# Tile-major storage of turned queries, keys and x, crossbar requests of two or three tiles, x of batch 2 by the crossbar, and a new written order

## The chip, the cores and the metric

The kernel runs on one core of a Trainium2 chip. The core has five engines that run their own instruction streams and meet at semaphores: TensorE (PE; its weight loads are shown apart as PEld), VectorE (DVE), ScalarE (ACT), GpSimd (POOL) and SyncE (SP). Work on data is done by the first three; here GpSimd and SyncE mostly issue DMA transfers. Everything an instruction touches lies in SBUF, the core's memory of 128 partitions, or in PSUM, eight banks into which TensorE writes. The metric is the device time of one run in microseconds.

## The reference

Attention with a window and a few global keys feeds a gated long convolution. Batch is 4, heads 8, sequence 768, head dimension 64, so the model width is 512.

```
scores = q k^T / 8 - slope[h] * dist        # keep = first 8 keys, or 0 <= i - j < 96
a      = softmax(where(keep, scores, -1e9)) # dist = 96 for a global key out of the window
x      = concat_heads(a v)                  # 4 x 768 x 512
x1, x2, x3 = split(x w_proj)                # 512 -> 3 * 512
x2     = irfft(rfft(x2) * rfft(filter))     # along the sequence, length 768
out    = (x1 * x2 * x3) w_out
```

## The kernel before

**Tiles of a batch.** The sequence is cut into seven key tiles. A key tile has 128 rows: 8 global keys and 120 keys of its own (`KL = 120`). Tile t's keys meet a band of at most 216 queries that begins at query 120 t; the widths are `EW`. Tiles are worked in three groups, `GRP = [(0, 1), (2, 3), (4, 5, 6)]`. Queries are loaded in six tiles of 128 rows. Four head pairs share the 128 partitions, 64 rows for each head of a pair, so that the scores of both heads run side by side on TensorE (`scores`, L798 to 835).

**Turning.** TensorE contracts over partitions, so queries, keys and the attention's result x have to be turned. This is done in three ways. For batch 0, `turned_pair` (L728) turns pairs of heads from contiguous loads. For batches 1 and 2, `turned` (L778) turns tile by tile on TensorE into a PSUM bank, and ScalarE or VectorE copies the bank into QT or KT. For batch 3, `crossed` (L764) has SyncE issue a DMA transpose (the crossbar) from SBUF to SBUF for each tile, 13 requests. x of batches 0 to 2 is turned on TensorE and copied out of PSUM, and x of batch 3 by 12 crossbar requests, two for each group and half of the heads (`transpose_x`, L895). `XB` and `XX` name the batches whose queries and keys, or whose x, go by the crossbar.

**Storage.** QT, KT and xT hold the head pair (or the chunk of 128 channels) as the outer dimension and the sequence inside it. xn, the attention's result before turning, is two buffers, one for each half of the heads.

**After the attention.** `gate` (L963) multiplies x with the first and last third of w_proj; for a batch whose x came by the crossbar its columns come in pieces of 120 out of tiles of 128 (L990, L993), for the others in 384 at a time (L988). `butterfly` (L920) folds x for the transform, `conv` (L1034) projects it (L1049), transforms it (`transform`, L705), multiplies it with the filter's spectrum (L1216 to 1234), transforms it back (L1136 to 1141), gates it and multiplies it with w_out (L1100); SyncE stores the result from one of six output buffers (L1107). The filter's spectrum is made once (`spectrum`, L635).

**Order.** The kernel first lists some 950 operations with what each reads and writes, and then issues them in an order written out in the string `ORDER`: number, engine letter (P, A, V, G for GpSimd, S for SyncE) and, for P, the PSUM banks. Each engine runs its part of that order strictly in sequence. Words such as `i1b0` are matmuls of no use that keep TensorE running in the front. The costs in `g.op(...)` were used to find such an order, and take no part in the run.

**Queues.** [...] SyncE issues stores, crossbar requests, and copies of the global rows within SBUF (`load_global`), in its own sequence.

Of the kernel before, what the change touches and what calls it, by code (L numbers as in the profile page):

```python
# [28 lines left out]
def act(n):  # L29
    return 0.06 + n / 1200.0  # L30
# [11 lines left out]
0V 34G 18S 30S i1b0 15V i1b0 21S 5G 35V i1b0 60V i1b0 59V 57V 10G 55V 7V i1b0 14V i1b0 24G 1V 56V 191A 8V i1b0 17V 61A  # L42
28G 190A i1b0 12A 20V i1b0 36V i1b0 19A 54V 58V 37G 214P0 13V 193A i1b1 29G 11V 215A i1b1 16V 192A i1b1 196A 25G 216V
204P1 22A 217V 38G 209P2 23V 26G 205A 219P0 39V 62V 63V i1b3 220A 52G 108P3 206V 210A 66P4 194A 207V 109A i1b5 27G
i1b5 211V 106P5 221V 42G 67V i1b1 i1b1 94P1 43G 212V 114P67 208A 110V 222V 92P4 213A 40G 95V i1b2 218A 111P23 223A
107A i1b0 41G 96V 64P0 93V i1b1 259G 115P 53V 224V 103P45 68V 65V 46G 195A 104P 112P 116A 80P1 199V 257G 9V 105A 81V
100P67 i1b0 i1b0 113A 101P 82V 225V 97P01 102A 6V 72P23 98P 232V 31A 73P 86P67 260G 99A 33S 117P45 226V 198V 74A 233V
78P0 118P 79A 75P23 234V 44G 76P 119A 32V 87P 235V 83P01 45G 77A i1b4 236V 69P45 256G 88A 70P 237V 84P 89P23 71A 258G
90P 238V 125P67 85A i1b4 227V 48G 126V 135P45 127V 91A 47G 120P01 136V 252P67 121V 267G 137V 130P23 253A 122V 241P4
254A 272G 138P5 131V 123P0 132V 249P67 266G 139V 352P1 251A 152P23 353V 273G 242A 133P7 250A 153V 157P45 268G 154V  # L50
124A 128P6 350P0 265G 158V 129A 155P1 159V 348P2 197A 354A 156A 49G 246P6 349V 160P4 351A 50G 244P5 134V 247A 161V
360P01 362P23 203V 271G 182V 361A 239P4 181V 140P67 274G 240A 175V 363A 174V 261G 143P01 177V 141A 202V 51G 245A
355P67 144V 275G 357P23 356A 377P5 375P4 176V 460G 358A 378V 414P6 165P01 184V 376A 264G 183V 415V 379A 277G 255V
380P45 385P67 381A 146P23 200V 185V 386A 178V 464G 142V 412P4 145V 186A 416P5 179V 162P67 476G 262S 180V 147A 417V
263S 413A 471G 148V 187V 387P23 418A 163A 149P45 359V 388A 243V 188V 289P6 270G 150A 189V 419P23 269G 290A 382P45 201V
279P7 151V 383A 389V 478G i1b6 420A 365P45 276G 281P6 166A 366V 367V 463G 280A 421P23 364V 426P01 282A 424P45 293P7
480G 422A 384V 283P6 425A 294V 461G 299P23 427A 167V 370P45 423V 477G 368P7 284A 171P01 369A 371V 472G 372V 300A
390P67 428V 462G 172A 395P45 164V 285P23 248A 469G 396V 173V 228P0 286A 391V 397V 291P1 470G 301V 229A 555P2 230A 392V
465G 434P45 292A 302V 231A 429P67 556A 468G 287V 168P01 430V 678G 557A 435V 431V 475G 551P2 436V 169A 373P3 553P6 664G
393P7 552A 374V 619P4 554V 398P5 295P01 394V 481G 620A 399V 580P2 288V 296A 563P45 663G 467S 565P67 581V 578P3 566A  # L60
466S 437P0 297V 667G 617P2 564A 170V 432P1 438V 686G 400P67 298V 618A 579V 682G 433A 309P2 567V 401A 681G 560P45
558P01 307P3 452V 310A 403P67 679G 561A 451V 685G 559A 305P2 402V 311P4 308A 453V 677G 303P5 404A 317P0 621V 454V
315P3 479G 306A 615P1 562V 406P67 318A 316A 670G 312A 616V 304A 455V 573P23 666G 407A 313P1 574V 405V 627P45 582A 456V
278G 314A 482P0 575V 628A 683G 408V 588P67 457V 483A 622P23 590P45 492P1 623A 474G 320V 319V 591A 409P23 665G 458V
493A 321V 674G 589A 459V 502P01 568P45 473G 322V 668S 503A 494P6 569V 323V 684G 410A 496P7 570V 495A 675G 324V 583P23
497A 624P45 592V 439P01 625A 676G 584A 504V 680G 585P45 626V 629P67 440A 571P2 484P3 673G 630A 411V 325V 498P01 586A
442P67 631V 762S 485A 326V 499A 486P3 760S 587V 443A 598P01 637P45 487A 599V 327V 761S 572A 445P67 600A 638V 639V 758S
488P23 441V 593P45 501V 489A 576P0 759S 333P1 328V 446A 632P23 594V 500V 334A 671S 595A 448P67 490V 669S 505V 784S
633V 336P1 444V 577A 634V 449A 640P4 601P0 491V 337A 768P23 596P5 641V 783S 769A 512P6 602V 508P7 597V 513A 765P01
509V 770P23 763P45 766A 786S 329V 635P6 506P7 771A 518P0 636V 510P1 785S 507V 764A 514P6 654V 606P23 511A 822S 519A  # L70
655V 515A 516P1 345P0 450V 517A 447V 821S 607A 772V 520P1 346A 794P67 787P23 608V 792P45 338S 521A 767V 342P0 793A
819S 656V 330P1 788A 522V 820S 778P45 343A 523V 603P23 331A 657V 795A 779V 658V 773P01 604A 612P67 332S 774V 780V 524A
672S 775V 339P4 613A 796V 828P01 340A 789P67 659V 825P23 605V 790A 341S 609P45 525V 829A 660V 526V 642P67 826A 781S
791V 4A 610A 823P23 776S 614V 830P01 3A 824A 611V 645P45 527V 831A 661V 782S 802P23 528V 643A 648P01 803V 529V 646A
335S 777S 804A 651P45 662V 644V 827V 797P67 649A 806S 700P2 798V 832V 799A 833P01 805S 647V 531V 689P3 701A 800S 702P6
# [1306 lines left out]
```

## Time and profile before

| what | us |
|---|---|
| median of 3 runs | 167.62 |
| lowest, highest run | 166.46, 171.16 |
| span of the profiled execution | 166.3 |
| busy: PE, DVE, ACT, POOL | 157.9, 151.4, 148.2, 73.8 |

The page of the profiled execution gives its span, from its first to its last instruction, and no other time of its own; the lowest of the runs is 0.2 us longer. The page has six parts: busy time by engine; the span in 40 slices; the DMA queues; the chain of work that ended last, followed back from the end; the costliest groups of instructions; and the DMA issues. In a row of a group stand the line of the kernel, the engine, the operation, what it writes and reads, the count, the busy time and the mean duration in ns, and then the idle time just before it with what ended it. Matmuls are pipelined: a row's duration of one matmul is longer than the distance between two, which the starts in the chain show.

### The profile page before, as it was taken

To read this page: it belongs to the slowest core of one execution; us is meant where nothing else is said; L and a number is where in the kernel's file an instruction comes from. 1 tells how busy PE (TensorE), PEld (TensorE's weight loads), DVE (VectorE), ACT (ScalarE), POOL (GpSimd) and SP (SyncE) were. 2 spreads that over 40 slices of the span, in tenths; PEclk is the share of its full clock that TensorE was granted. 3 is DMA by queue.
4 is the path that set the end of the run, shared out by engine and by line. 5 is a ranking of instruction groups with operands and counts; after the bars stand their busy time and mean duration, and the time that the engine had idled before them with its cause. 6 is when DMAs were issued, how large, how long until landed. Compare 5 with 4: busy or idle time off the path is not lost.

```text
span 166.3 us, 4460 instructions
## 1 busy us (share of the span) xinstructions
PE 157.9 (95%) x1735; PEld 98.2 (59%) x1735; DVE 151.4 (91%) x348; ACT 148.2 (89%) x268; POOL 73.8 (44%) x94
## 2 busy tenths in 40 slices
PE   6999998999999999999999999999999699999991
PEld 2356566856536687765566685566555454585440
DVE  6898699899979999999999999999999979999960
ACT  3999995998999979999999999999997579998972
POOL 7896399999699979999730000000000000000000
PEclk9999999999999999999999999999999999999999
DMA  5999999999999999999999656423133135000696
GB/s 151 146 138 194 160 161 153 170 170 176 175 162 149 152 148 125 137 145 139 159 152 144 122 97 155 85 79 110 40 73 112 68 129 189 0 4 0 252 348 221
DMA packets 90365, 22.84 MB, mean 137 GB/s; under 512 B 81504, under 2 KB 87016, under 8 KB 90344
## 3 DMA queue, kind: packets, MB, share of 16 engines
q0 software_dynamic: 74880, 12.46, 100.9%
q1 hardware_dynamic: 15464, 10.10, 22.2%
q8 instruction: 13, 0.21, 0.5%
q14 instruction: 8, 0.07, 0.1%
HBM read 25.69 MB, written 6.29 MB: 192 GB/s over the span
## 4 chain that ended last, share of the span: by engine, by line
PE 50%; DMA 16%; DVE 15%; POOL 13%; issue 2%; SPq 1%; ACT 1%; ACTq 0%; POOLq 0%; DVEq 0%
PE bank L988 10%; PE bank L1100 10%; PE bank L1049 7%; DMA g<-in_moe_filter_fft_dram 6%; PE bank L990 5%; POOL kn L330 4%; DMA vn<-in_v_dram 4%; POOL qn L330 4%; DMA vn<-vn 3%; PE bank L811 3%; DVE xn L885 2%; DMA out_dram<-ot 2%; PE bank L861 2%; DVE E L835 2%; PE bank L866 2%
## 5 line engine op out<-in xcount | busy, mean ns | idle before, releaser
L823 ACT ACTIVATE E<-bank 128x864 f16<-128x864 f32 x48 | 40.5, 909 | 1.2 <-PE bank L811 1.1
L988 PE MATMUL bank<-xT,w 128*128 128x384 f16 x192 | 34.7, 326 | 0.0
L318 ACT ACTIVATE x<-bank 128x768 f16<-128x768 f32 (+2 forms) x31 | 25.5, 830 | 2.4 <-PE bank L988 1.0
L330 POOL DMA_DIRECT2D vn<-in_v_dram x28 | 25.6, 923 | 2.2 <-DMA w<-in_moe_w_proj_dram 1.6
L988 PEld LDWEIGHTS <-w 128*128 128x128 f16 x192 | 17.7, 98 | 11.1 <-issue 0.3
L1100 PE MATMUL bank<-wo,y 128*128 128x512 f16 (+1 forms) x100 | 22.5, 370 | 0.0
L330 POOL DMA_DIRECT2D kn<-in_k_dram x24 | 21.8, 910 | 1.5 <-DMA wo<-in_moe_w_out_dram 1.0
L330 POOL DMA_DIRECT2D qn<-in_q_dram x21 | 18.4, 881 | 5.7 <-DMA g<-in_moe_filter_fft_dram 4.2
L835 DVE TENSOR_TENSOR E<-E,mask 128x1728 f16<-128x1728 f16 x18 | 18.8, 1048 | 0.0
L318 ACT ACTIVATE ot<-bank 128x512 f32<-128x512 f32 (+1 forms) x23 | 12.9, 599 | 3.5 <-PE bank L1100 1.8
L885 DVE TENSOR_TENSOR xn<-bank,rc 128x512 f16<-128x512 f32 (+1 forms) x20 | 15.5, 789 | 0.3
L861 PEld LDWEIGHTS <-E 128*128 128x128 f16 x224 | 14.1, 97 | 2.8 <-DVE E L835 0.7
L1049 PE MATMUL bank<-w,xab 128*128 128x512 f16 x64 | 15.6, 379 | 0.0
L861 PE MATMUL bank<-vn,E 128*128 128x65 f16 x224 | 15.3, 193 | 0.2 <-DMA vn<-vn 0.2
L1100 PEld LDWEIGHTS <-y 128*128 128x128 f16 x100 | 9.5, 98 | 10.0 <-issue 0.3
L866 PE MATMUL bank<-vn,E 128*128 128x65 f16 x192 | 15.1, 193 | 0.0
L314 ACT CAST ab<-bank 128x512 f16<-128x512 f32 x23 | 13.7, 607 | 0.7 <-PE bank L1049 0.6
L866 PEld LDWEIGHTS <-E 128*128 128x128 f16 x192 | 13.2, 97 | 0.9
L811 PE MATMUL bank<-QT,KT 64*128 64x216 f16 (+2 forms) x224 | 13.3, 241 | 0.4 <-DVE pp L1229 0.4
L314 ACT CAST eo<-bank 128x384 f16<-128x384 f32 x30 | 12.9, 523 | 0.5 <-PE bank L1141 0.5
L314 ACT CAST X<-bank 128x1024 f16<-128x1024 f32 x12 | 12.2, 1032 | 0.0
L811 PEld LDWEIGHTS <-KT 64*128 64x128 f16 x224 | 7.9, 94 | 6.6 <-issue 5.2
(187 smaller groups left out, 363.0 us busy)
## 6 DMA issues: line engine op xcount, KB each, us to landing
out_dram<-ot SPq DMA_DIRECT2D x23, 256.0 KB
vn<-in_v_dram POOLq DMA_DIRECT2D x28, 120.0 KB, 6.1
kn<-in_k_dram POOLq DMA_DIRECT2D x21, 120.0 KB, 6.4
qn<-in_q_dram POOLq DMA_DIRECT2D x18, 128.0 KB, 6.1
w<-in_moe_w_proj_dram POOLq DMA_DIRECT2D x4, 256.0 KB, 6.8
g<-in_moe_filter_fft_dram POOLq DMA_DIRECT2D x1, 768.0 KB, 10.6
kn<-in_k_dram POOLq DMA_DIRECT2D x3, 192.0 KB, 4.3
qn<-in_q_dram POOLq DMA_DIRECT2D x3, 192.0 KB, 5.0
```

The costliest lines, as they stand in the source:

```text
L314: {"A": nc.scalar.copy, "V": nc.vector.tensor_copy, "G": nc.gpsimd.tensor_copy}[e](out, in_)
L318: self.nc.scalar.mul(out, in_, c)
L330: return self.g.op(eng, 0.57 + 0.00035 * nbytes[0] if eng == "G" else 0.5, lambda _: e.dma_start(dst, src), w=w, r=r, nbytes=nbytes, name= ...
L811: nc.tensor.matmul(bs[hh].f32()[:, off:off + w], self.KT[hs, hp, P * m:P * m + P], self.QT[hs, hp, KL * m:KL * m + w], start=(off == 0 and ...
L823: g.op("A", act(864), lambda _: nc.scalar.activation(eo, bs[0].two()[:, :, 0:432].rearrange("p h (m w) -> p h m w", m=2), Act.Exp, scale=s ...
L835: g.op("V", dve(1728, 2), lambda _: nc.vector.tensor_mul(ep, ep, mk), r=[("mask", h) for h in range(hs.start, hs.stop)] + ([("mask0", hp - ...
L861: nc.tensor.matmul(o[:, n, hh], ef[:, at:at + P], vt[:, t, 2 * hp + hh, 0:D + 1], start=first, stop=(t == 0), skip_group_check=True)
L866: nc.tensor.matmul(o[:, n, hh], ef[:, at:at + P], vt[:, t - 1, 2 * hp + hh, 0:D + 1], start=False, stop=True, skip_group_check=True)
L885: nc.vector.tensor_mul(to, o[:, :, :, 0:D], rc.to_broadcast([P, 2, 2 * nt, D]))
L988: nc.tensor.matmul(bk.f32()[:, 0:h], w, self.xT[:, c, lo:lo + h], **kw)
L1049: nc.tensor.matmul(bk.f32(), src[:, c], w[:, c, DM:2 * DM], start=(c == 0), stop=(c == 3))
L1100: nc.tensor.matmul(bk.f32()[:, 0:n], y[:, c, P * t:P * t + P], self.wo[:, c, ns], start=(c == 0), stop=(c == 3))
```

## The change

- QT, KT and xT get the tile as the outer dimension, then the head pair or chunk, then 128 columns. xn becomes one buffer with the tile outside and all heads inside.
- Queries are loaded in seven tiles that begin every 120 rows and overlap by eight (the last has 48 rows), as the key tiles do. A score of 216 columns then reads two query tiles, 120 and 96 columns, in two matmuls. Batches 1 and 2 turn a seventh query tile. Batch 0's copies of turned queries are split in two instructions.
- A crossbar request covers all tiles of a group: three requests for queries (3, 2, 2 tiles) and three for keys (2, 2, 3) of batch 3.
- x of batch 2 goes by the crossbar too (`XX = (2, 3)`); for each group one request takes both halves of the heads. TensorE's transposes of it and the copies go; its gates and butterfly read tiles of 120 columns. As batch 1 has stored x in the other layout, the requests of batch 2 are put after all readers of batch 1's x (`past`).
- h1, half of whose slots were unused, shrinks from six to four.
- `ORDER` is written anew: 931 operations in place of 949, 88 on GpSimd in place of 85, 49 on SyncE in place of 62, 20 useless matmuls in place of 26. In it the load of the filter stands at place 58 of GpSimd's entries (it was the 11th), the spectrum comes after five of batch 0's projections, and attention of batches 1 and 2 comes earlier against the convolution of batch 0.

```diff
 ORDER = """
...
-    XX = (3,)
+    XX = (2,3)
+    QG = [(0, 1, 2), (3, 4), (5, 6)]
...
-        self.qn = t("qn", [P, 6, H, D])
+        self.qn = t("qn", [P, 7, H, D])
-        self.QT = t("QT", [P, 4, S])
-        self.KT = t("KT", [P, 4, 7 * P])
+        self.QT = t("QT", [P, 7, 4, P])
+        self.KT = t("KT", [P, 7, 4, P])
-        self.xn = [t(f"xn{i}", [P, 2, 7, 2, D]) for i in range(2)]
-        self.xTt = t("xT", [P, 4, 7, P])
-        self.xT = self.xTt.rearrange("p j t c -> p j (t c)")[:, :, 0:S]
+        self.xn = t("xn", [P, 7, 4, 2, D])
+        self.xTt = t("xT", [P, 7, 4, P])
+        self.xT = self.xTt.rearrange("p t j c -> p (t j c)")[:, 0:4 * S].rearrange("p (j s) -> p j s", j=4)
...
     def load_q(self, b, t):
-        src = self.q[b, :, P * t:P * t + P, :].rearrange("h p d -> p h d")
-        self.load("G", self.qn[:, t], src, [("qn", t)], (1024, 256), f"q{t}")
+        n = min(P, self.S - KL * t)
+        src = self.q[b, :, KL * t:KL * t + n, :].rearrange("h p d -> p h d")
+        self.load("G", self.qn[0:n, t], src, [("qn", t)], (8 * n, 256), f"q{t}")
...
     def crossed(self, what, ts, buf):
-            o, i = dst[:, :, P * t:P * t + P], buf[:, t].rearrange("p h d -> p (h d)")
+        o = (self.QT if what == "q" else self.KT)[:, ts[0]:ts[-1] + 1].rearrange("p t i c -> p (t i) c")
+        i = buf[:, ts[0]:ts[-1] + 1].rearrange("p t h d -> p (t h d)")
...
             for m in m0:
-                w = self.EW[m]
-                for hh in range(2):
-                    hs = slice(64 * hh, 64 * hh + 64)
-                    nc.tensor.matmul(bs[hh].f32()[:, off:off + w],
-                                     self.KT[hs, hp, P * m:P * m + P],
-                                     self.QT[hs, hp, KL * m:KL * m + w],
+                for x, w in ((m, min(KL, self.EW[m])), (m + 1, self.EW[m] - KL)):
+                    for hh in range(2 if w > 0 else 0):
+                        hs = slice(64 * hh, 64 * hh + 64)
+                        nc.tensor.matmul(bs[hh].f32()[:, off:off + w], self.KT[hs, m, hp],
+                                         self.QT[hs, x, hp, 0:w],
...
         if self.b in self.XX:
-            for i in range(2):
-                g.op("S", 0.3 + 0.25 * len(ts), lambda _, i=i: nc.sync.dma_start_transpose(
-                    out=self.xTt[:, 2 * j + i, ts[0]:ts[-1] + 1],
-                    in_=self.xn[j][:, i, ts[0]:ts[-1] + 1].rearrange("p t h d -> p (t h d)")),
+            if j == 0:
+                if c == 0:
+                    ks = [("xT", x, y, i) for x in range(2) for y in range(3) for i in range(2)]
+                    self.past = {o for k in ks for o in g.readers.get(k, ())} if self.b - 1 not in self.XX else set()
+                return
+            g.op("S", 0.3 + 0.25 * len(ts), lambda _: nc.sync.dma_start_transpose(
+                out=self.xTt[:, ts[0]:ts[-1] + 1].rearrange("p t i c -> p (t i) c"),
+                in_=self.xn[:, ts[0]:ts[-1] + 1].rearrange("p t i h d -> p (t i h d)")),
+                r=[("xn", 0, c), ("xn", 1, c)], w=[("xT", x, c, i) for x in range(2) for i in range(2)],
+                nbytes=(128 * len(ts), 1024), name="crossx", after=self.past)
             return
```

More of the change, by code (lines that the diff above doesn't have):

```diff
@@ L47 @@
[L47 to L51, printed above, removed]
@@ L691, in packed @@
         g.op("P", 2 * pe(512), run, acq=[b, b2], r=keys + ["twin"], name="fwd")
-        g.op("AV", self.evac(512), lambda e: self.times(e, h1[:, s], b.f32(), sc), use=[b],
+        g.op("AV", self.evac(512), lambda e: self.times(e, h1[:, s - 2], b.f32(), sc), use=[b],
              w=[("h", s, 1)])
@@ L780, in turned @@
         b = g.bank()
+        rows = [min(P, self.S - KL * t) if what == "q" else P for t in ts]
         def turn(_):
@@ L912, in run @@
                     o = step * i + KL * n
-                    nc.tensor.transpose(tx[:, o:o + P], self.xn[j][:, i, t], self.ident)
-        g.op("P", 0.0559 * 2 * len(ts), run, acq=[b], r=[("xn", j, c), "ident", "xpad"], name="trx")
+                    nc.tensor.transpose(tx[:, o:o + P], self.xn[:, t, 2 * j + i], self.ident)
+        g.op("P", 0.0559 * 2 * len(ts), run, acq=[b], r=[("xn", j, c), "ident"], name="trx")
         dst = self.xT[:, 2 * j:2 * j + 2, self.Q0[c]:self.Q0[c] + W]
```

174 lines of the change are left out of this document (91 added, 83 removed).

## The prediction

> **What bounds the kernel now.** I read the page first, then the chain of work that ended last, then the stretches of 10 us, and last the rows of the lines that the diff touches.
>
> ```profile
> span 166.3 us, 4460 instructions
> PE 157.9 (95%) x1735; PEld 98.2 (59%) x1735; DVE 151.4 (91%) x348; ACT 148.2 (89%) x268; POOL 73.8 (44%) x94
> PE 50%; DMA 16%; DVE 15%; POOL 13%; issue 2%; SPq 1%; ACT 1%; ACTq 0%; POOLq 0%; DVEq 0%
> ```
>
> The chain is TensorE for half of the span, and DMA and GpSimd for 29%. VectorE and ScalarE are busy for 91% and 89%, so there is no engine on which work can be put for nothing. The stretches say where each of these binds (columns: stretch, length, then busy time and count of PE, PEld, DVE, ACT, POOL, clock, DMA share, GB/s):
>
> ```profile
> 0.00:10.00 10.00, 8.59 (x67) 3.45 (x69) 7.57 (x44) 7.28 (x18) 8.66 (x22) 1.00 0.82 150
> 20.00:30.00 10.00, 9.19 (x173) 6.94 (x168) 9.44 (x23) 7.97 (x13) 9.82 (x12) 1.00 2.14 160
> 80.00:90.00 10.00, 10.00 (x122) 6.47 (x121) 9.96 (x17) 10.00 (x21) 3.32 (x4) 1.00 2.58 144
> 130.00:140.00 10.00, 8.49 (x53) 4.27 (x52) 8.43 (x16) 7.78 (x17) 0.00 (x0) 1.00 0.31 114
> ```
>
> GpSimd, which issues every load, is nearly full in the front and done before 90 us; in the middle PE, DVE and ACT are all full; and from 130 to 140 us PE lacks 1.5 us. That hole has a name:
>
> ```profile
> 126.98 0.57 SPq L1107 DMA_DIRECT2D out_dram<-ot  x1
> 130.91 0.60 ACT L318 ACTIVATE ot<-bank 128x512 f32<-128x512 f32 x1 [1.69 <-DMA out_dram<-ot]
> ...
> 114.30 12.63 SPq L900 DMA_TRANSPOSE xT<-xn  x9
> ...
> L900 SPq DMA_TRANSPOSE xT<-xn x12: 1180/1200/2282, 109.8 to 125.7; - x12
> L773 SPq DMA_TRANSPOSE QT<-qn x6: 1193/1214/1306, 85.5 to 100.9; - x6
> PE bank L1139 <- ACT ot L318: 1.5, 1, 1.5
> ```
>
> SyncE issues nine crossbar requests of x in one row, 12.63 us, and a store that stands behind them goes out only at 126.98. ScalarE waits 1.69 us for its buffer, and TensorE 1.5 us for ScalarE.
>
> **The change on TensorE.** It is the engine of the chain in the middle and at the end, so I sum it there. The rows (start, time, what):
>
> ```profile
> 61.32 0.22 PE bank L913 x4
> 98.31 1.30 PE bank L988 x8
> 135.45 0.15 PE bank L990
> 135.63 0.16 PE bank L990
> 142.05 1.22 PE bank L990 x8
> 60.88 0.45 PE bank L785 x8
> ...
> 111.21 0.55 PE L811 MATMUL bank<-QT,KT 64*128 64x216 f16 x12
> L811 PE MATMUL bank<-QT,KT x224: 181/252/263, 14.0 to 111.6; 64*128 64x216 f16 x80, 64*128 64x168 f16 x16, 64*128 64x48 f16 x16
> ```
>
> *Removed:* the 28 transposes of x of batch 2 (seven tiles by four). Four take 0.22 us, so 28 take 1.54 us.
>
> *Gates of batch 2.* Eight gates of eight matmuls of 384 columns are 8 x 1.30 = 10.40 us. In the crossbar's layout four are of 360 columns, 4 x 1.22, and four have 360 and 48: from one 360 to the next are 0.18 us (135.45 to 135.63), so eight are 1.42. Together 4.88 + 5.68 = 10.56 us: +0.16.
>
> *Scores.* A score of 216 columns becomes one of 120 and one of 96, because a query tile now holds 120 used columns. Per head 13 matmuls stand for 7, so 6 x 32 = 192 more, which run in pairs: 96 more pairs, the same columns. From 384 to 360 columns a matmul falls from 1.30/8 = 0.1625 to 1.22/8 = 0.1525 us, 2.4 columns per ns. The 12 scores at 111.21 are six pairs of 216, 168, 48, twice; from the first start to the last are 0.55 - 0.18 = 0.37 us, over five pairs of 816 columns, 0.34 us. What is left is 6 ns a pair. 360 columns at that rate are 0.150 of the 0.1525 us, so 2.5 ns is the low end. 96 pairs cost 0.24 to 0.58 us; I take 0.4, between.
>
> *The seventh query tile.* Batches 1 and 2 turn 48 rows more, four transposes each. At most that is a full transpose, 0.45/8, for eight: 0.45 us; at least the 48 columns of the gate, 0.18 - 0.15: 0.2 us. I take 0.2, the row of that width.
>
> TensorE together: -1.54 + 0.16 + 0.4 + 0.2 = **-0.8 us**.
>
> **Beside TensorE.** For the middle:
>
> ```profile
> L314 DVE COPY xT<-bank 128x480 f16<-128x480 f16 x7 | 2.7, 399 | 0.2 <-PE bank L913 0.2
> L314 ACT COPY xT<-bank 128x480 f16<-128x480 f16 x5 | 3.0, 605 | 0.4 <-PE bank L913 0.3
> L931 DVE TENSOR_TENSOR xab<-xT 128x1536 f16<-128x1536 f16 x4 | 3.6, 951 | 0.0
> L935 DVE TENSOR_TENSOR xab<-xT x2: 751/752/752, 128.2 to 129.2; 128x1152 f16<-128x1152 f16 x2
> L936 DVE TENSOR_TENSOR xab<-xT x2: 299/300/302, 128.9 to 129.9; 128x288 f16<-128x288 f16 x2
> L937 DVE TENSOR_TENSOR xab<-xT x2: 200/200/201, 129.1 to 130.1; 128x96 f16<-128x96 f16 x2
> L314 DVE COPY QT<-bank 128x512 f16<-128x512 f16 x2 | 0.8, 418 | 0.0
> ```
>
> Six copies of x out of PSUM go, 6 x 0.40 on DVE or 6 x 0.605 on ACT: 2.4 to 3.6 us. The butterfly of batch 2 reads three pieces instead of one: 2 x (0.752 + 0.300 + 0.200 - 0.951) = +0.6. Two small query copies come, at most 2 x 0.42, and four copies of batch 0 are split, each with a second instruction near that of L937: +0.8 both times. So 0.2 to 1.4 us less on two engines together; I count it at nothing, since PE's own work covers it. If it did not, it would be a gain. The writes of xn get another order of dimensions, which no row shows; I take zero, and 20 such writes a tenth longer would be 1.6 us.
>
> **The crossbar.** Requests fall from 25 to 12: six for queries and keys of batch 3, three for x of batch 2, three for x of batch 3. A request now covers two or three tiles, 8 to 12 blocks of 128x128, while the rows have 2 or 3 blocks at a median of 1.200 us and 4 blocks at 1.214. Twice the blocks cost 1% more. So I take 1.2 to 1.3 us each, 15 us of SyncE in place of 31; the other end is 0.3 us per block. Each request waits for its last tile and, for x, for both head groups. All three x requests of batch 2 stand behind the last gate of batch 1, which is new (`past`):
>
> ```profile
> 82.27 0.40 PE L913 MATMUL bank<-ident,xn 128*128 128x128 f16 x4
> 91.23 1.46 PE L988 MATMUL bank<-xT,w 128*128 128x384 f16 x8
> ```
>
> Now x of batch 2 starts to be turned at 82.27, though batch 1's last gate runs only until 92.69. Behind these requests on SyncE stand the two copies of global value rows of batch 3 and then the stores of batch 0; values of batch 3 and the output buffers wait for them. Three requests are 3 x 1.25 = 3.8 us after the gate; the order puts all of batch 1's gates ahead, and other batches' matmuls cover it. Nothing is counted. Of the 1.5 us hole at 130 us I count **-1.0**: stores no longer stand behind nine requests, but what is late next there is the butterfly and its projection.
>
> [...]
>
> **The front.** The written order moves the 1.5 MB load of the filter from the 11th of 85 to the 58th of 88 of GpSimd's entries, and with it the spectrum: seven DVE steps, six transforms with their copies. GpSimd also gets three query loads.
>
> ```profile
> 8.27 10.61 DMA g<-in_moe_filter_fft_dram
> ...
> 3.41 1.76 POOL L330 DMA_DIRECT2D kn<-in_k_dram  x2
> ...
> 19.41 0.90 POOL L330 DMA_DIRECT2D qn<-in_q_dram  x1 [4.23 <-DMA g<-in_moe_filter_fft_dram]
> L330 POOL DMA_DIRECT2D qn<-in_q_dram x21: 629/906/1069, 6.1 to 82.7; - x21
> L690 PE MATMUL bank<-g,p x4: 376/378/379, 26.6 to 28.6; 128*128 128x512 f16 x4
> ```
>
> GpSimd stalls 4.23 us behind the filter now, ahead of batch 1's loads; that much the front can gain. The three loads add at most 3 x 0.906 = 2.7 us, the last of them behind everything that waits early. Against it, the spectrum's vector work leaves a front where DVE has 2.4 us of room in 10 and goes where it has 0.04. Ends: -4.2 and +6 (below). I take 0, for the same work is only done at another time.
>
> **Sum.** -0.8 - 1.0 + 0 = -1.8 us on the profiled execution, 164.5. Its span is 166.3; the runs are 166.46 to 171.16, median 167.62, so a run lies 0.2 to 1.3 us over it without the highest. With 0.7 that gives **165.2 us**, 1.4% under the median. Own range 163.3 to 167.0. Two per cent is about what a measurement of this kernel tells from no change.
>
> **Rivals.**
>
> *The front gets shorter* (0.26). Loads of batches 0 and 1 come up to 4.2 us sooner, TensorE starts its attention sooner, and the stall behind the filter meets a time when loads are ahead. The row of 4.23 speaks for it; that PE's busy time in the front includes filler matmuls, so it has room, does too. With 3 of the 4.2 us: 165.2 - 3 = 162.2.
>
> *The filter comes too late* (0.24). This is the slower side. Ahead of it stand 52 loads at 0.9 us and 3.4 us of setup (first load at 3.41): issued at about 50 us, landed 10.6 later, at 60. Now the first transform runs at 26.6, 7.7 us after the landing at 18.9, so then it would be at 68. The matmuls that the order puts ahead of it (attention of batches 0 and 1, scores of 2, five projections) are, by my count of the order, about what PE has done now some 0.7 us after it turns x of batch 1 at 61.32, say by 62. PE, in order, would stand 6 us, and DVE has no room to catch up: 165.2 + 6 = 171.2. It decides as soon as the six transforms start later than PE is through, by the load or by the sums on DVE. Against it: the sums need not take 7.7 us.
>
> *Requests cost by the block* (0.08). Then x of batch 2 adds 28 blocks at 0.3, 8.5 us of SyncE ahead of values of batch 3, the 1.0 us does not come, and x lands 2 us later per group of three tiles: 165.2 + 1.0 + 1 = 167.2.
>
> **How the numbers follow.** The forecast has 0.42. Under 164.3 (2% under 167.62) lie the shorter front and 0.04 of the forecast: 0.30. Over 171.0 lies most of the late filter: 0.20. The rest, 0.50, is within 2%. The range leaves out the far part of the two outer rivals: 161.5 to 171.0.
>
> **What would show it.** Right: no L913 after 70 us; crossbar requests on SyncE of 1.2 to 1.3 us whatever their tiles; no wait of ScalarE for a store past 120 us; PE's busy time by matmuls about 1 us less. Front: the stall on the filter gone from GpSimd's waits, first scores before 14 us. Wrong: transforms of the spectrum that wait for DVE or the filter, a request of 2.4 us or more, values of batch 3 waiting for their global rows, or PE waiting for an x copy. Longer xn writes would also make it wrong.

## The result and the profile after

The changed kernel is slower: 175.12 us (median of 4 runs, 174.8 to 175.57) against 167.04 for the kernel before on the same chip; the ratio is 1.056, with a 95% interval of 1.051 to 1.062. The forecast was 165.2. The profiled execution of the changed kernel took 175.57 us; its span is 173.8 against 166.3, so there are 7.5 us to find. (Runs of one kernel fall into a faster and a slower group; the ratios compare the faster runs, and where a trace is of a slower one, as those of no_v3, new_xx3, v_after and store_first are, only waits and starts are read from it.) Three rows and the clock of the page after:

```profile
span 173.8 us, 4867 instructions
PE 161.2 (93%) x1933; PEld 102.0 (59%) x1933; DVE 151.1 (87%) x346; ACT 151.0 (87%) x271; POOL 75.6 (43%) x97
PEclk9999999999999999999987999999999999999997
PE 41%; POOL 27%; DMA 22%; issue 5%; DVE 2%
```

In the chain of work that ended last, TensorE has 41% instead of 50%, and GpSimd and DMA together have 49% instead of 29%. VectorE and ScalarE are busy for 151.1 and 151.0 us, against 151.4 and 148.2 before, in a longer span. So the kernel waits more for data, and the clock row says that TensorE was slowed near the middle. The stretches find the place (columns as before: stretch, length, busy time and count of PE, PEld, DVE, ACT, POOL, then clock, DMA share, GB/s):

```profile
85.00:90.00 5.00, 1.30 (x12) 0.57 (x9) 4.86 (x10) 1.59 (x4) 0.90 (x1) 1.00 1.80 89
90.00:95.00 5.00, 4.87 (x62) 2.97 (x63) 0.00 (x0) 3.52 (x5) 0.00 (x0) 0.66 1.83 144
130.00:140.00 10.00, 10.00 (x76) 5.95 (x75) 9.87 (x20) 8.84 (x17) 0.00 (x0) 1.00 0.42 116
```

From 85 to 90 us TensorE works for 1.30 us of 5; before, the stretch from 80 to 90 was full. From 90 to 95 it is busy, but at a granted clock of 0.66. From 130 to 140, where the kernel before lacked 1.5 us, it is now full. The waits name what was missing at 85:

```profile
PE bank L815 <- DMA QT<-qn: 3.8, 1, 3.8
PE bank L815 <- DMA KT<-kn: 1.5, 1, 1.5
```

Scores (L815) wait for turned queries and turned keys, which are those of batch 3, the batch that goes by the crossbar. The timeline, SyncE's requests first and then two rows of scores, shows when they were asked for and when they were used:

```profile
72.77 1.34 SPq L774 DMA_TRANSPOSE KT<-kn  x1
74.28 4.54 SPq L774 DMA_TRANSPOSE QT<-qn  x1
78.99 5.20 SPq L774 DMA_TRANSPOSE KT<-kn  x1
84.35 8.81 SPq L774 DMA_TRANSPOSE QT<-qn  x2
93.32 4.73 SPq L774 DMA_TRANSPOSE KT<-kn  x1
99.67 6.88 SPq L908 DMA_TRANSPOSE xT<-xn  x3
...
63.33 0.59 PE L815 MATMUL bank<-QT,KT 64*128 64x96 f16 x18
90.13 0.46 PE L815 MATMUL bank<-QT,KT 64*128 64x120 f16 x6 [3.83 <-DMA QT<-qn]
```

The last scores of batch 2 are done by 63.9 us; the first of batch 3 come at 90.13. The same places in the timeline of the kernel before, with its first request:

```profile
81.79 0.55 PE L811 MATMUL bank<-QT,KT 64*128 64x216 f16 x10
83.71 1.66 SPq L773 DMA_TRANSPOSE KT<-kn  x1
94.51 0.36 PE L811 MATMUL bank<-QT,KT 64*128 64x216 f16 x4 [0.39 <-DVE pp L1229]
```

There batch 2's scores end at 82.3 and batch 3's begin at 94.51, with a wait of 0.39 us that is not for a transfer. The rows of the lines that the change touches (minimum, median and maximum in ns; first and last start in us):

```profile
L774 SPq DMA_TRANSPOSE KT<-kn x3: 1341/4728/5202, 72.8 to 93.3; - x3
L774 SPq DMA_TRANSPOSE QT<-qn x3: 3004/4542/5636, 74.3 to 90.2; - x3
L908 SPq DMA_TRANSPOSE xT<-xn x6: 1233/1410/2955, 99.7 to 131.1; - x6
L922 PE MATMUL bank<-ident,xn x56: 217/219/230, 28.9 to 63.1; 128*128 128x128 f16 x56
L815 PE MATMUL bank<-QT,KT x416: 179/203/298, 13.7 to 112.0; 64*128 64x120 f16 x63, 64*128 64x96 f16 x54, 64*128 64x48 f16 x22
```

Requests of queries and keys take 3 to 5.6 us, but for the first. The three of x of batch 3, past 120 us, when no load moves, take 1.23 to 1.25 us for two tiles and 1.40 for three. And the chain of after steps over exactly this stretch:

```profile
77.70 15.59 DMA vn<-in_v_dram
93.32 11.97 DMA KT<-kn
```

A load of v issued at 77.70 lands 15.6 us later (the median of such loads on the page is 6.5), and the last key request, begun at 93.32, lands 12 us later.

**A balance of TensorE's work.** I add up the matmuls by their starts, at the distance that the prediction found (columns at 2.4 per ns, and 2.5 ns), without the useless ones. The sum is 141.1 us before and 140.4 after.

```
us           before   after   difference
up to 85      67.2     64.7     -2.5      the front
85 to 110     23.6     16.9     -6.7      the crossbar stage
110 to end    50.3     58.8
whole        141.1    140.4     -0.7
```

In the span: 2.5 behind at 85 us, less 0.7 that need not be done, is 1.8; plus 6.7; minus 1.0 that comes back later, where the hole at 130 us was (from 110 us to the end of the span 56.3 us for 50.3 of work before, 63.8 for 58.8 after): +7.5. The two waits of the crossbar stage, 3.8 and 1.5 us, and the 1.7 that a clock of 0.66 costs in 5 us make 7.0, near the 6.7 of the table. At its first scores of batch 3 the kernel before has 65.1 us of work left, and the changed one 74.5: TensorE begins these scores 4.4 us sooner, with 9.4 us more still to do. It asks for their queries sooner still, at 86.30 us, when its wait begins, against 94.51.

### The profile page after: what moved, and what is told of

It reads as the page before. It is cut to its first block, busy times and chain, and to the rows that moved or that the text cites. A ratio compares the mean times of both kernels' runs of the same rounds, so it can differ in the third digit from the quotient of the medians.

```text
span 173.8 us, 4867 instructions
## 1 busy us (share of the span) xinstructions
PE 161.2 (93%) x1933; PEld 102.0 (59%) x1933; DVE 151.1 (87%) x346; ACT 151.0 (87%) x271; POOL 75.6 (43%) x97
## 4 chain that ended last, share of the span: by engine, by line
PE 41%; POOL 27%; DMA 22%; issue 5%; DVE 2%
PE bank L999 11%; PE bank L1113 10%; POOL kn L329 9%; DMA vn<-in_v_dram 9%; POOL vn L329 9%; POOL qn L329 8%; DMA KT<-kn 7%; DMA w<-in_moe_w_proj_dram 6%; PE bank L1062 6%; PE bank L309 4%; PE bank L704 2%; PE bank L1152 1%; PE bank L864 1%; PE bank L869 1%; PE bank L1002 1%
## 5 line engine op out<-in xcount | busy, mean ns | idle before, releaser
L329 POOL DMA_DIRECT2D vn<-in_v_dram x28 | 26.5, 959 | 5.7 <-DMA qn<-in_q_dram 4.7
L1113 PE MATMUL bank<-wo,y 128*128 128x512 f16 (+1 forms) x100 | 23.4, 371 | 0.1
L999 PE MATMUL bank<-xT,w 128*128 128x360 f16 x128 | 23.3, 314 | 0.0
L997 PE MATMUL bank<-xT,w 128*128 128x384 f16 x128 | 23.0, 326 | 0.3 <-ACT x L317 0.2
L329 POOL DMA_DIRECT2D qn<-in_q_dram x24 | 20.7, 877 | 4.6 <-DMA w<-in_moe_w_proj_dram 2.4
L815 PE MATMUL bank<-QT,KT 64*128 64x120 f16 (+2 forms) x416 | 15.6, 210 | 5.4 <-DMA QT<-qn 3.8
L815 PEld LDWEIGHTS <-KT 64*128 64x128 f16 x416 | 11.1, 96 | 11.9 <-issue 8.6
L997 PEld LDWEIGHTS <-w 128*128 128x128 f16 x128 | 11.9, 98 | 7.8
L999 PEld LDWEIGHTS <-w 128*128 128x128 f16 x128 | 12.2, 97 | 7.1
L313 ACT CAST ab<-bank 128x512 f16<-128x512 f32 x24 | 14.4, 625 | 1.8 <-PE bank L1062 1.8
L1062 PE MATMUL bank<-w,xab 128*128 128x512 f16 x64 | 15.6, 382 | 0.2 <-ACT xT L313 0.2
L864 PEld LDWEIGHTS <-E 128*128 128x128 f16 x224 | 13.9, 97 | 1.4
```

Source lines behind the costliest of these rows:

```text
L313: {"A": nc.scalar.copy, "V": nc.vector.tensor_copy, "G": nc.gpsimd.tensor_copy}[e](out, in_)
L329: return self.g.op(eng, 0.57 + 0.00035 * nbytes[0] if eng == "G" else 0.5, lambda _: e.dma_start(dst, src), w=w, r=r, nbytes=nbytes, name= ...
L815: nc.tensor.matmul(bs[hh].f32()[:, off:off + w], self.KT[hs, m, hp], self.QT[hs, x, hp, 0:w], start=(off == 0 and not near), stop=True, sk ...
L864: nc.tensor.matmul(o[:, n, hh], ef[:, at:at + P], vt[:, t, 2 * hp + hh, 0:D + 1], start=first, stop=(t == 0), skip_group_check=True)
L997: nc.tensor.matmul(bk.f32()[:, 0:h], w, self.xT[:, c, lo:lo + h], **kw)
L999: nc.tensor.matmul(bk.f32()[:, 0:360].rearrange("p (t r) -> p t r", t=3), w, self.xTt[:, 3 * s:3 * s + 3, c, 0:KL], skip_group_check=True, ...
```

## The experiments

The theory to begin with: in the new order the requests run **beside loads**, and the two slow each other (*clash*). The rivals: a request of two or three tiles is slow by itself (*size*); the new order costs its time whatever the transfers do (*order*). What the trace holds of DMA packets, counted by start over 2 us, shows the first of these plainly:

```
kernel        us       load packets   crossbar descriptors (mean ns)
before        84-86       2401             19  (18)
before        86-88       1375            340  (34)
before        90-92         25           1638  (25)
after         72-74       2395              0
after         76-78        222            479  (59)
after         82-84        254            257  (54)   230 of the loads are 1 KB, of w_out
after         86-88        325            303 (136)
after        106-108         0           2016  (18)
```

One tile is 512 descriptors of 256 bytes. Alone, loads go at 2400 packets in 2 us and a request at some 2000 descriptors; from 86 to 88 us in the changed kernel, together, each goes at about a seventh of that. When the first request starts, 5,202 load packets are still to come before, and 13,559 after. The last of them starts at 90.4 us before, and at 104.7 after. The kernel before had the clash too, for four microseconds.

**old_order**: the changed code, in the order of before.

```diff
-5G 0V 15A 14V 7V 13V ...
+0V 34G 18S 30S i1b0 15V ...      (before's words, renumbered; a request after its last tile)
```

> The changed code with the order of the kernel before: the same storage, merged requests, x of batch 2 by the crossbar and seven query tiles, but every operation at its old place (a merged request at the place of its last part, the new ones beside their neighbours). Clash theory (crossbar requests and loads in flight together slow each other): requests start after the last load is issued, so each takes 1.2 to 1.6 us of SyncE, and the sum of the prediction holds: span 163.5 to 167, ratio 0.98 to 1.00. Size theory (a request of 8 to 12 blocks is slow by itself, or x of batch 2 by the crossbar comes too late): requests of 3 us or more, span 169 to 175. Order theory (the late filter and the new order of everything cost it): as the clash theory in the time, but with the front alone to blame, to be told apart by the other runs.

171.13 us, ratio 1.031 (1.018 to 1.044). SyncE's timeline:

```profile
85.01 5.14 SPq L775 DMA_TRANSPOSE QT<-qn  x1
90.25 0.71 SPq L330 DMA_DIRECT2D vn<-vn  x1
91.01 0.69 SPq L330 DMA_DIRECT2D kn<-kn  x1
93.36 1.24 SPq L909 DMA_TRANSPOSE xT<-xn  x1
94.72 1.83 SPq L775 DMA_TRANSPOSE QT<-qn  x1
```

The first request of queries, issued while loads run, takes 5.14 us; those from 93.36 on take 1.2 to 1.8. TensorE waits 2.5 us for queries, until 97.21. The order is not the whole loss. The 0.98 to 1.00 that the clash theory gave did not come: two requests still begin while loads run, and the last load is through only at 95.7 us. From 91.7 to 93.36 SyncE stands still: x of batch 2 is at the head of its queue and not ready, with queries and keys behind it.

**no_v3**, **by_tile** and **cross_late** change the new order's transfers: the first leaves out the seven loads of v of batch 3, the second splits each request of queries or keys by tile, the third lists batch 3's v as something a request reads.

```diff
+            if b == self.B - 1: (no load)                                        # no_v3
-   nc.sync.dma_start_transpose(out=o, in_=i)
+   for x in range(n): nc.sync.dma_start_transpose(out=o[:, 4 * x:4 * x + 4],    # by_tile
+                                                  in_=i[:, 512 * x:512 * x + 512])
-   r=[(what + "n", t) for t in ts] + ...
+   r=[(what + "n", t) for t in ts] + ... + [("vn", 1, t) for t in range(7)]     # cross_late
```

> The changed kernel without the seven loads of the values of batch 3 (its result for batch 3 is computed with the values of batch 1); order unchanged. These are the loads in flight beside the requests for queries and keys. Clash theory: requests of 1.2 to 2 us, TensorE's waits for QT and KT (5.3 us) nearly gone, clock 1.0, span 165 to 168. Size theory: requests stay at 3 to 5.6 us, span 172 to 174. Order theory: span 171 to 173.

> The changed kernel with each request for queries and keys of batch 3 issued as one request for each tile (14 in place of 6), at the same place. Size theory: requests back to 1.2 us each, queries land by 86, span 167 to 170. Clash theory: the 14 requests together take as long as the six (28 us of SyncE) or a little longer, span 173 to 177.

> The changed kernel, in which the requests for queries and keys of batch 3 wait until the seven loads of values of batch 3 have landed; the rest of the order as it was. Clash theory: the last load lands at 88 to 92 in place of 105, requests take 1.2 to 1.4 us, all keys and queries land by 100 in place of 105; TensorE waits longer for the first and not for the last, span 171 to 174. Size theory: requests of 3 us or more from 90 on, span 180 and more.

no_v3: two runs, 167.2 and 173.64 us, too few for a ratio; the trace is of the longer. In it requests still take 3.0 to 5.6 us until 88.9, as long as other loads run, but for the first; behind that all take 1.23 to 1.43. The span of the shorter run, 165.5 us at a clock of 1.00, lies where the clash theory put it, but it is one run. by_tile: 173.21, ratio 1.042 (1.019 to 1.066); its 14 requests take 1.2 to 2.8 us, and TensorE waits 4.3 us for queries. So *size* is out: the same tiles one by one come no sooner. cross_late: 173.4, ratio 1.043 (1.025 to 1.062). The list of what an operation reads sets only the order of issue, and as no data are shared, SyncE did not wait: the first request stands at 72.63 as ever. It tested nothing but issuing v a little earlier, and serves as a second look at the changed kernel: requests of 3.4 to 4.8 us, a wait of 2.8.

**fence_new** and **fence_old** make SyncE really wait, by a small copy that reads the seven tiles of v.

```diff
+        def sent(_):
+            if what == "k" and ts[0] == 0:
+                nc.sync.dma_start(self.fence, self.vn[1][NG:NG + 1, :, 0, 0:4])
+            nc.sync.dma_start_transpose(out=o, in_=i)
```

> The changed kernel, but SyncE first copies four values of each of the seven v tiles of batch 3 into a scratch row, ahead of its first crossbar request, so that no request starts before the last load has landed; GpSimd issues these seven loads ahead of their old places. Nothing is left out. Clash (requests and loads in flight at once slow each other): the last load lands before 92 us, the requests begin there and take 1.2 to 1.5 us each, whatever their tiles, all six are through 10 us after the fence; TensorE then waits for the last of them instead of for slow ones, and the time is 171 to 174 us. Size (a request of two or three tiles is slow by itself): each still takes 3 to 5 us behind the fence, 175 us or more. Order alone (the new order costs it whatever the transfers do): requests as with clash, but 175 us.

> The changed code in the order of before (171.1 us in its run) with the same fence ahead of the first request; nothing is left out. Clash: the query request that took 5.14 us there, begun at 85 us when the last load landed at 95.7, is gone, all requests take 1.2 to 1.5 us, the last load lands at 89 to 91 us as before, and the time falls by the 2 to 3 us that TensorE waited for queries: 168 to 169.5 us. Size: a request of queries stays above 3 us and the time at 171. If the fence puts the requests too late (they begin at 91 in place of 83), clash by its price alone: 171 again, but with requests of 1.2 us.

fence_new: 178.41 us, ratio 1.056 (1.045 to 1.068). SyncE's timeline, the wait and three stretches:

```profile
88.07 1.35 SPq L778 DMA_TRANSPOSE KT<-kn  x1
89.53 1.46 SPq L778 DMA_TRANSPOSE QT<-qn  x1
92.88 2.65 SPq L778 DMA_TRANSPOSE QT<-qn  x2
```

```profile
PE bank L820 <- DMA QT<-qn: 8.4, 1, 8.4
```

```profile
85.00:90.00 5.00, 0.17 (x1) 0.00 (x0) 3.70 (x7) 0.59 (x1) 0.00 (x0) 0.75 0.50 48
90.00:95.00 5.00, 1.47 (x25) 1.20 (x26) 0.00 (x0) 0.53 (x1) 0.00 (x0) 0.50 1.03 194
95.00:100.00 5.00, 5.00 (x46) 2.62 (x45) 1.02 (x2) 3.82 (x6) 0.00 (x0) 0.72 0.80 150
```

The transfers did as *clash* says: the last load at 86.7 instead of 104.7, requests of 1.3 to 1.7 us, all six landed by 98.8. The time did not: it is no better, because now TensorE stands 8.4 us until 93.53. My price was wrong; I had taken the requests to be ready before TensorE asked. fence_old: 174.52 us in the middle of four runs (172.46 to 176.79); the two shortest, 172.46 and 173.39, are too few for a ratio with an interval. The slow query request is gone (1.47 us in place of 5.14), but it starts at 93.49 instead of 85.01, and TensorE waits 2.9 us for queries and 1.8 for ScalarE. By these two, about 1.03 times the kernel before on that chip, a clash avoided by waiting costs as much as the clash (old_order: 1.031).

**filter_early**: only the filter's load goes back to its old place.

```diff
-... 49G 37G 48G ...   52G (58th)
+... 49G 52G 37G 48G ...
```

> The changed kernel with the load of the filter back at the 11th place of GpSimd's entries and all else in the new order; nothing is left out. If the moved filter cost the front its 2.5 us (TensorE had 64.7 us of work done at 85 us where before had 67.2), 172.5 to 173.5 us. If the front pays for other loads that now stand later, the filter ahead of them makes it worse: 176 to 178 us. If the front is no matter beside the crossbar stage: 175.

172.34 us, ratio 1.019 (1.007 to 1.031). The middle of the runs that the ratio compares, 172.02 us, over that of the kernel before on the same chip, 167.38, is 1.028, inside this interval but well above its middle. TensorE waits for a query load early, and not for queries in the crossbar stage:

```profile
PE bank L787 <- DMA qn<-in_q_dram: 2.7, 1, 2.7
```

```profile
85.00:90.00 5.00, 5.00 (x95) 4.10 (x94) 4.96 (x12) 4.48 (x11) 0.00 (x0) 1.00 1.69 148
90.00:95.00 5.00, 5.00 (x71) 3.08 (x64) 4.93 (x9) 4.71 (x8) 0.00 (x0) 1.00 2.68 114
```

The front is not faster, it is slower: by 85 us TensorE has done 3.4 us less than in the changed kernel. Its requests are as slow (2.8 to 5.7 us, but for the first). But TensorE comes to batch 3's scores when they can be had (89.69 us), with no idle stretch and a clock of 1.00. What it loses is lost early and not a second time. So the number came near one expectation (172.5 to 173.5) and its reason did not hold.

**probe** measures the disputed cost by itself: four one-tile requests in the kernel before, where only loads run.

```diff
+                    for i in range(4):
+                        self.nc.sync.dma_start_transpose(
+                            out=self.h1[:, 1 + 2 * (i % 2)]..., in_=self.fwd[:, 4:8]...)
```

> The kernel before, with four requests more of SyncE behind its copies of the global rows of batch 1, near 47 us, each turning 128 x 512 values of a constant into slots of h1 that nobody reads; nothing is left out. In that stretch loads run alone, at some 2,400 packets in 2 us, and no request stands beside them in the kernel before. Clash: each of these one-tile requests takes 2.5 to 5 us in place of 1.2, and the loads fall to below 1,200 packets in 2 us as long as they run; what is lost of 8 to 12 us of loads comes later, the last load lands 3 to 8 us after 90.4, and the kernel takes 169 to 174 us. If requests and loads do not slow each other: 1.2 us each, loads unchanged, 167.5 us.

168.96 us, ratio 1.012 (1.006 to 1.018), just under the range. Its packets over 2 us:

```
us       load packets   crossbar descriptors (mean ns)
46-48       2440              0
48-50       1018            390  (46)
50-52       1126            505  (43)
54-56       2424              0
56-58       1025            473  (48)
58-60       1334            531  (30)
```

Loads fall to less than half, and two tiles take more than 4 us to move, where 1024 descriptors alone would take one (an estimate, from the 2016 in 2 us above). The four cost about 5,300 load packets, 4.4 us at 2400 in 2 us; the last load starts 2.9 us later, where 3 to 8 were expected. But SyncE's rows are 1.2 to 1.6 us each, not the 2.5 to 5 that I expected: the row of one tile is **not** the time until it lands. Longer rows are, in the changed kernel, those of larger requests beside loads (3 to 5.6 us), and in by_tile those of some one-tile requests behind others (up to 2.8 us).

**old_xx3**, **new_xx3** and **old_qk_first** take x of batch 2 apart from the rest: off the crossbar in the order of before, off it in the new order, and behind all queries and keys in the order of before.

```diff
-    XX = (2,3)
+    XX = (3,)                        # old_xx3, new_xx3
-757S 756S ... 578S 775S 600S 638S 776S 806S 807S
+757S 756S ... 775S 776S 806S 807S 578S 600S 638S   # old_qk_first
```

> Storage by tile and requests of two or three tiles alone: the changed code with x of batch 2 turned on TensorE again (XX is batch 3 only), in the order of before. Nothing is left out. If the loss of the run in the order of before (171.1 us) came from x of batch 2, whose requests wait for x at the head of SyncE's queue with those of queries and keys behind them: 167.5 to 169 us, the storage's own price of 0.4 to 0.8 us on TensorE. If it came from the merged requests beside the last loads (a query request took 5.14 us): a request of three query tiles still takes 4 to 5 us and the time is 170 to 171.

> The changed kernel in the new order, with x of batch 2 turned on TensorE again at the places of its requests; nothing is left out. If the new order loses its time while TensorE waits for the keys and queries of batch 3, whose requests come ahead of those of x: they take 3 to 5 us and land at 90 as in the changed kernel (175.1 us), and the 1.5 us of TensorE's work fall partly into its waits: 174.5 to 176.5. If the requests of x beside the last loads are what costs: 170 to 172.

> The changed code in the order of before, with all six requests of queries and keys ahead of the three of x of batch 2 in SyncE's queue; TensorE's gates and the folding of batch 2 that need them go behind. Nothing is left out. If x of batch 2 at the head of the queue held up the queries and keys: the first scores of batch 3 at 94 to 95.5 us in place of 97.2, 168.5 to 170 us against 171.1. If TensorE then waits as long for x of batch 2: 171 to 172.

old_xx3: 169.21 us, ratio 1.013 (1.005 to 1.021); a query request of 4.68 us at 84.61, and a wait of 1.5:

```profile
PE bank L816 <- DMA QT<-qn: 1.5, 1, 1.5
```

Storage and merged requests alone cost a good per cent, 2.2 us by the ratio: the 1.5 of this wait and the 0.6 that the prediction had for scores and query tiles on TensorE would make 2.1. The rest of old_order's loss goes with x of batch 2, as far as two ratios can say whose intervals overlap. new_xx3: ratio 1.053 (1.043 to 1.063), with much the same wait for queries, 3.6 us; x of batch 2 matters little in the new order. old_qk_first: 177.24, ratio 1.062 (1.057 to 1.068), worse than either expectation: the first scores came at 96.89 (97.21 in old_order), and then x was late.

```profile
PE bank L1000 <- DMA xT<-xn: 3.3, 1, 3.3
```

**no_v23** leaves out the 14 loads of v of batches 2 and 3 in the changed kernel.

```diff
+            if b >= 2: (no load)
```

> The changed kernel without the loads of v of batches 2 and 3 (14 loads of 120 KB; their rows are those of batches 0 and 1), so that the loads end some 12 us earlier. If the new order loses because it asks for the keys and queries of batch 3 while loads still run: the last load lands near 77, the requests take 1.2 to 2 us, the first scores of batch 3 come at 80 to 84 us without a wait of TensorE over 1 us, and the time is 166 to 169 us. If requests are slow by their size or the loss has nothing to do with the loads: 173 or more.

167.51 us (10 runs), ratio 1.004 (1.001 to 1.007): of the loss of 5.6% 0.4 are left. The timeline and two stretches:

```profile
69.16 1.34 SPq L777 DMA_TRANSPOSE KT<-kn  x1
70.66 4.46 SPq L777 DMA_TRANSPOSE QT<-qn  x1
75.29 1.37 SPq L777 DMA_TRANSPOSE KT<-kn  x1
76.83 2.65 SPq L777 DMA_TRANSPOSE QT<-qn  x2
79.64 1.44 SPq L777 DMA_TRANSPOSE KT<-kn  x1
...
85.23 0.27 PE L818 MATMUL bank<-QT,KT 64*128 64x120 f16 x4
```

```profile
85.00:90.00 5.00, 5.00 (x74) 3.15 (x73) 4.93 (x10) 4.66 (x7) 0.00 (x0) 1.00 0.01 3
90.00:95.00 5.00, 5.00 (x63) 3.12 (x62) 4.90 (x10) 4.71 (x7) 0.00 (x0) 1.00 0.13 31
```

The loads end at 74.6 us. The request that still meets them takes 4.46, the four behind it 1.2 to 1.4, all land by 83, and TensorE begins batch 3's scores at 85.23 without a wait. Same storage, same merged requests, same order: nearly the whole loss hangs on the loads that still run when batch 3 is asked for. What the kernel before would gain without these 14 loads was not run.

**v_after** and **v_after_fe** ask whether it is the clash or the amount: the seven loads of v of batch 3 wait until all six requests have landed, the second with the filter's load early.

```diff
+                def behind(e, run=op.fn):
+                    for f, src in zip(self.fence, (self.QT, self.KT)):
+                        self.nc.gpsimd.dma_start(f, src[0:1, :, 0, 0:4])
+                    return run(e)
```

> The changed kernel, but GpSimd first copies a few values of all seven tiles of QT and KT into scratch rows, ahead of its first load of v of batch 3, so that these seven loads start only when all six requests have landed. Nothing is left out. If mutual slowing of requests and loads is the larger part: the requests are through by 90 us, the first scores of batch 3 stand at 84 to 87 us in place of 90.1, the last load lands at 96 to 99 in place of 104.7, and the time is 170 to 173 us. If the new order needs more transfers in this stage than any sequence can bring: TensorE now waits for v of batch 3 in place of the queries, 174 us or more.

> The same, with the load of the filter at the 11th place of GpSimd's entries (172.3 us without the rest). Nothing is left out. Mutual slowing: 168 to 171 us. Too many transfers for the stage: TensorE waits for v, 172 us or more. If the early filter helped only because it made TensorE later, so that it meets the keys with more work in hand: the gain of 2.8 us against the run without it is gone here, and both take the same.

v_after: four runs, 170.0, 174.43, 176.63 and 176.96 us, which give no ratio, so its time decides nothing; its trace is of the longest. v_after_fe: 174.9 us, ratio 1.047 (1.031 to 1.062). The waits of v_after and, below them, of v_after_fe:

```profile
PE bank L1007 <- DMA xT<-xn: 2.7, 1, 2.7
PE bank L823 <- DMA QT<-qn: 2.5, 1, 2.5
...
PE bank L795 <- DMA qn<-in_q_dram: 2.6, 1, 2.6
PE bank L1007 <- DMA xT<-xn: 1.4, 1, 1.4
```

In v_after the scores begin at 88.58 instead of 90.13, the v loads are over only at 108.6, and meet x of batch 2, for which TensorE waits. In this trace the loss moved on. So in none of the traces of the three sequences (loads first, together, requests first) does the new order bring its transfers in time. But the run of 170.0 us had a mean clock of 0.994, where the traced one had 0.979, so it may have had less of these waits; that no sequence can do it is not shown. v_after_fe fits the second expectation by its time and not by its reason: TensorE never waits for v. It waits for a query load in the front, as filter_early does, and comes to batch 3's scores at 89.40 us. By the count of the balance it does 22.4 us of work from 85 to 110 us, and filter_early 23.1, against 16.9 in the changed kernel and 23.6 before: these two lose their time in the front. Whether filter_early's gain is lost when v comes behind the requests cannot be said, since v_after, the run to compare with, has no ratio.

**store_first** tries to have the hole at 130 us filled without the rest: in the kernel before, two stores go ahead of eight requests of x.

```diff
-806S 805S 800S 801S 837S 836S 842S 841S 347S 550S 344S
+347S 344S 806S 805S 800S 801S 837S 836S 842S 841S 550S
```

> The kernel before with two stores of batch 0, whose outputs are ready near 105 us, put ahead of the last eight requests of x of batch 3 in SyncE's queue, and nothing else. Nothing is left out. If TensorE's 1.5 us before 130.91 us hang on the store that went out at 126.98: ScalarE waits for no store past 120 us, TensorE has no wait over 0.5 us there, and the time is 0.8 to 1.5 us less, a ratio of 0.991 to 0.995. If the folding and projection of batch 3, which the requests of x now reach 1.1 us later, are late next: no gain, ratio 0.998 to 1.004.

169.91 us, ratio 1.023 (1.016 to 1.029), slower than either expectation.

```profile
PE bank L1049 <- DVE xo L944: 2.2, 1, 2.2
DVE xab L935 <- DMA xT<-xn: 2.5, 1, 2.5
```

The wait for the store is gone; in its place VectorE waits 2.5 us for x, and TensorE 2.2 for the folding. With twelve requests of x of batch 3 in the queue either the stores or x is late; with three, in the changed kernel, neither is. TensorE waits 0.7 us more than in the kernel before; what the rest of the 2.3% is stays open. No kernel that was run beats the one before.

## Why the prediction was wrong

*TensorE, -0.8.* Right: 141.1 to 140.4. This count uses the prediction's own rates, so it confirms the number of matmuls and not the price of one. L922 turns no x after 63.1 us, as foretold.

*Beside TensorE, nothing.* Right in the sum: TensorE waits for no copy, folding or write of xn by more than 0.6 us. Wrong in the working: VectorE and ScalarE together are busy for 302.1 us after and 299.6 before, 2.5 us more, where 0.2 to 1.4 less was worked out. Why is open.

*The crossbar, "1.2 to 1.3 us each ... Nothing is counted".* **This is the step that failed.** Of its two halves the size was nearly right: 1.233 us for two tiles and 1.40 for three where no load runs, so a tile more, four blocks, costs 0.17 us, and the rival of 0.3 us a block is refuted. What was wrong was to price a request by SyncE's row and to leave out its company. In the kernel before, the row at 83.71 is 1.66 us long, but the first 512 descriptors, as many as that request has, are through only at 89.2. And I followed what the new order puts **behind** the requests on SyncE, and not when it **asks** for what they bring. That is the missing term: 6.7 us between 85 and 110, where 1.2 was the price and 0 the sum. The change itself says that attention of batches 1 and 2 comes earlier; then TensorE comes to batch 3's sooner too, while GpSimd, which issued loads until 84 us before, has no less to load.

The probe shows what I should have weighed there: with requests of SyncE beside them, GpSimd's loads fall from 2440 packets in 2 us to 1018, by more than the crossbar's 390 descriptors would take at their pace alone (0.4 us, an estimate at 2000 in 2 us).

*The hole at 130 us, -1.0.* Right in the changed kernel: 10.00 of 10 busy, no wait of ScalarE for a store, and 1.0 us in the balance. "What is late next there is the butterfly and its projection" is what store_first met.

*The front, 0.* Inside its bounds but the wrong value: 2.5 us of work behind at 85 us. The first scores stand at 13.7 us, and GpSimd no longer stalls behind the filter, but behind other loads in its place: 2.4 us for a load of w_proj, until 62.24 us, and 4.7 for a query load, until 86.97. *The filter comes too late*, the rival that ended at 171.2, has the right side, and with 171.2 the nearest of the rivals' times, but that is luck: the first transform stands at 68.8 us, as it said, and TensorE does not wait for it. What the late place costs by itself cannot be read from filter_early, whose front loses more by another wait. In no_v23, with fewer loads in the front, TensorE is still 1.4 us behind the kernel before at 85 us by the same count, and the kernel as a whole stands at 1.004.

*The signs.* "A request of 2.4 us or more" was the sign of error that came true, for a reason that was on no list: no rival had a wait for batch 3's keys and queries. So the range, up to 171.0 us, had no case for it either.

## What to carry to other kernels

A transfer's row on the engine that issues it is not its time to arrive (before, 1.66 us against 5.5 for the first key request); look for who uses the data, and when, and what else is in flight until then. Before you bring forward work that needs the last loads, add up what the DMA engines still have to move at that moment (here 13,559 packets and 7,168 descriptors, in place of 5,202 and 6,656): an order that leaves the busiest engine without other work while they move loses that time (here waits of 3.8 and 1.5 us). And a fence shows that two things disturb each other, but it is no cure where the time is lacking (fence_new: 1.056, as without it).

## What was not expected of the hardware

**Loads and crossbar requests slowed each other by more than they share.** In the probe, 2,048 descriptors, which alone would take 2 us (2016 do from 106 to 108 us in the changed kernel), cost the loads 4.4 us. In the changed kernel, 13,559 packets would take 11.3 us at 2400 in 2 us (an estimate, and some 3 us more for w_out's larger packets: before, 1,604 packets in the 4 us from 76 to 80, where they run), and 7,168 descriptors 7.2 us at 2000: 18 to 22 us one after the other. Together they took 31.9 (72.8 to 104.7). fence_new, one after the other, has both through by 98.8. Why they slow each other is not known from these runs. Alone, the requests are not the slower kind: 2016 descriptors of 256 bytes in 2 us are 258 GB/s, more than the 125 to 210 that the rows of GB/s on the pages of before and after show while loads run alone. Beside loads, the 303 from 86 to 88 us in the changed kernel are 39 GB/s.

**The long waits were paid again in the clock.** In the changed kernel TensorE stands for 3.8 us, until 90.13, and its granted clock is 0.66 from 90 to 95 us: 0.50 from 89.97 to 93.39 us, and 1.00 in the stretches before and behind. That is 3.4 us at half speed, or 5 x 0.34 = 1.7 us, on top of the 3.8. In fence_new, where it stands for 8.4 us, it is 0.75, 0.50 and 0.72 in three stretches of 5. In no_v23 and filter_early, without a wait there, it is 1.00. A shorter wait was followed by the same: in old_order TensorE stands for 2.5 us, until 97.21, and from 98.17 to 101.58 the clock is 0.50. In old_xx3, after 1.5 us, it stays at 1.00.
